# Turning the value sums back at the end of the odd visit instead of in the middle of the even one

## The chip, the core and the metric

The kernel runs on one core of a Trainium2 chip. The metric is the device time of one execution in microseconds (us); lower is better. The kernel before took 2076.41 us (median of 3 runs, 2075.64 to 2079.05).

## What is computed

Four layers act on one sequence of 2048 rows of 640 numbers, in single precision: a Fourier mixing layer, a sliding-window attention layer, and the same two again. Each adds to its input:

```python
x = x + A(layernorm(x));  x = x + B(layernorm(x))      # twice
# A: y = dft_seq_re @ (x @ dft_hid_re.T) - dft_seq_im @ (x @ dft_hid_im.T)
# B, with H = 32 heads of Dh = 20 and a window of 256 keys:
qkv = x @ wqkv
scores = einsum("bhqd,bhkd->bhqk", q, k) * Dh ** -0.5
scores = where((i - j >= 0) & (i - j < 256), scores, -1e9)
o = einsum("bhqk,bhkd->bhqd", softmax(scores), v);  y = o @ wo
```

The change concerns layer B alone, which the kernel runs twice (function `attention`).

## The kernel before

**Numbers.** Single-precision operands of the large products are split into two 16-bit parts, and three products of parts are added up, so one product over 640 inner elements is 15 matmuls of 128 rows. The matmuls of the probabilities with the values, and two transposes behind them, are single precision throughout.

**Visits.** `attention` walks over *visits*, numbered by `G` in the loop at L1315. A visit handles one tile of 128 queries and two pairs of heads; two visits in a row (an even and an odd `G`) share the same heads. Every matmul goes through the helper at L126, and inside `attention` each one is tied to the one issued before it (`in_turn`), so the tensor engine runs them in exactly the order in which the Python code calls them. That order in one visit is:

1. `scores` for the oldest key tile, into the tile `sk` (even and odd alike);
2. `by_key`: the scores once more with keys on the partitions, for a visit eight earlier, also into `sk`;
3. `scores` for the two nearer key tiles, into `sq`. Steps 1 to 3 are 24 small matmuls on 62 rows of the array;
4. in an odd visit `hand_on`: a transpose of the row maxima `tops` through a bank `pf` (the scalar engine copies it to `ht`);
5. in an even visit `back(n)` (L1244): two single-precision transposes of `pvs` (the value sums of four heads) into a bank `pf`;
6. in an odd visit `values(n, part)` (L1223): 32 matmuls of `v` with the probabilities `ptq` into a bank `pf`, which the scalar engine then copies to `pvs` (L1242);
7. `run_unit` (L1068): the *fill*, usually 15 matmuls of 128 rows that belong to other work (projections of later blocks, of 256 or 320 columns; the output product `bo`, `ot` of 320 columns), into a bank `pf`.

Value sums are made at lag `VALUE_LAG` = 11 visits (odd) and turned back at `BACK_LAG` = 12 (the even visit behind it).

**Banks.** All the `pf` tiles of steps 4 to 7 come from one pool of two banks (`new_f`, L207). Whoever takes a bank waits until its last user's result was read out: by the scalar engine (`ht`, `pvs`, `qf` L365, `v` L881) or by the vector engine (`o` L1259, `x` L935).

**The vector engine.** Per visit it masks and reduces two tiles of scores (`largest`, L1148: COPY_PREDICATED L1155 and TENSOR_REDUCE L1157, twice). Behind `back`'s transposes it takes a reciprocal (`r`, L1258) and a product (`o`, L1259), from which GpSimd writes two parts `os` (L1261, L1262). `in_line("dve")` ties an instruction behind the last one noted in `marks["dve"]`; before, only the masks and reductions note themselves there. Between these stand the *slow steps* of layer norms (lines 139 to 166), one in an even visit and two in an odd one, and the sums of output units (L935).

When the last heads of a block are turned back, output units are queued for `OUT_STEPS[0]` = 4 steps (two visits) after the current one, and the turning of `os` into `ot` (a DMA on SyncE's queue) likewise.

Of the kernel before, what the change touches and what calls it, by code (L numbers as in the profile page):

```python
# [15 lines left out]
OP = mybir.AluOpType  # L16
AX = mybir.AxisListType

S, D, H, DH, P = 2048, 640, 32, 20, 128
# [26 lines left out]
BACK_LAG = 12  # L46
# [26 lines left out]
def body(ctx: ExitStack, tc: tile.TileContext, x_in, cmat, whid, wqkv, wo, out):  # L73
    nc = tc.nc
# [749 lines left out]
    def attention(layer, proj, dst, final):  # L824
        with ExitStack() as st:
# [293 lines left out]
            TOP, PT, topped, marks = {}, {}, [None], {}  # L1119
# [103 lines left out]
            def values(n, part):  # L1223

                b, k = divmod(n, NP // 2)
                q = PT[n]
                if part == 0:
                    PVS[n] = new_f().rearrange("p (a b) -> p a b", a=4)
                pv = PVS[n]
                j = 2 * b  # L1230
                for kt, cols, sel in (((j, slice(0, 2), slice(2, 5, 2)), (j - 2, slice(0, 1), slice(0, 1))),
                                      ((j - 1, slice(0, 2), slice(1, 4, 2)), (j + 1, slice(1, 2), slice(5, 6))))[part]:
                    if kt < 0:
                        continue
                    for h in range(4):
                        hh = 4 * k + h
                        matmul(pv[32 * h:32 * h + 32, cols], VS_[kt][:, VS * hh:VS * hh + 32], q[:, h, sel],
                                         start=kt == j, stop=kt == j + 1, tile_position=(0, 32 * h), skip_group_check=True)
                if part:
                    del PT[n]  # L1240
                    PVS[n] = sb.tile([P, 2, P], F32, tag="pvs", name="pvs", bufs=2)
                    nc.scalar.activation(PVS[n], pv[:, :2], AF.Copy)  # L1242

            def back(n):  # L1244
                b, k = divmod(n, NP // 2)
                t = PVS.pop(n)
                pv = new_f().rearrange("p (a b) -> p a b", a=4)
                for m in range(2):
                    transpose(pv[:, 2 + m], t[:, m], idf)
                pbv = pv[:, 2:].rearrange("p m (h e) -> p (m h) e", e=32)  # L1250
                if k == 0:
                    flush(("out", b - 3))
                    OS[b] = sb.tile([P, 2, 2, D], F16, tag="os", name="os", bufs=3)
                r = sb.tile([P, 8], F32, tag="r", name="r", bufs=2)
                cs = slice(4 * k * DH, 4 * (k + 1) * DH)
                o = sb.tile([P, 2, 4 * DH], F32, tag="o", name="o", bufs=2)
                hi, lo = (OS[b][:, :, m, cs] for m in range(2))
                nc.vector.reciprocal(r, pbv[:, :, DH])  # L1258
                nc.vector.tensor_tensor(o.rearrange("p m (h e) -> p (m h) e", e=DH), pbv[:, :, :DH],  # L1259
                                        r.unsqueeze(2).to_broadcast([P, 8, DH]), op=OP.mult)  # L1260
                nc.gpsimd.tensor_copy(hi, o)  # L1261
                nc.gpsimd.tensor_tensor(lo, o, hi, op=OP.subtract)  # L1262
                last = b == NBQ - 1
                d1 = (k + 1) * 4 * DH // P
                if last and d1 > k * 4 * DH // P and (d1 > 2 or k > LAST_FROM):
                    for m in range(2):
                        step0 = max(now[0] + LAST_STEPS[0], NG + 2 * KEY_LAG if m else LAST_STEPS[1] if d1 < ND else 0)
                        fill.append(Unit(step0, last_out(2 * b + m, lastd[0], d1), "last", NS + 2 * d1 + m, [(2 * b + m - 2, 2)]))
                    lastd[0] = d1
                elif k == NP // 2 - 1 and not last:  # L1270
                    for m in range(2):
                        i = 2 * b + m
                        at, due, kind = now[0] + OUT_STEPS[0] + OUT_STEPS[2] * m, 2 * NP * (b + 2) + OUT_STEPS[1], ("out", b)
                        need = [(i - 2, 2)] if i > 1 else []
                        outs.append((at, need, partial(out_turn, i)))
                        fill.append(Unit(at, out_tile(i), kind, due + 3 * m + 2, [(i, 1)] + ["wo"] * (layer == 0)))
# [33 lines left out]
            def due(G, lag):  # L1310
                n, m = divmod(G - lag, 2)
                return n if m == 0 and 0 <= n < NG // 4 else None

            wanted, x2s, normed_at = [], [], [-FREE_STEPS]
            for G in range(NS // 2 + 1):  # L1315
                now[0] = g = 2 * G
                b, r = divmod(g, 2 * NP)
                if g == NG:
                    floor.append(loads[-1])
                if g < NG:  # L1320
                    if r == 0:
                        flush(("qk", b))
                        if b == 0:
                            queue_qk(1)
                            queue_v(1)
                keyed = 0 <= G - KEY_LAG < NG // 2
                if g < NG:
                    scores(G, (0,))
                if keyed:
                    by_key(G - KEY_LAG)  # L1330
                if g < NG:
                    scores(G, (2, 1))
                if g < NG:
                    largest(G, 0)
                if keyed:
                    probabilities(G - KEY_LAG, 1)
                if g < NG:
                    largest(G, 1)
                    if G % 2:
                        part_tops(G // 2)  # L1340
                if keyed:
                    probabilities(G - KEY_LAG, 0)
                n = due(G, HAND_LAG)
                if n is not None:
                    hand_on(n)
                n = due(G, BACK_LAG)
                if n is not None:
                    with in_line("dve"):
                        back(n)
                c = 2 if g == 0 else b + 3  # L1350
                if g < NG and c < NBQ and (g == 0 or r == X2_STEP):
                    wanted.append(c)
                if wanted and x2s and g >= x2s[0] + 4 * (g > 0):
                    slow.append(rows_norm(wanted.pop(0), x2s.pop()))
                    x2s.clear()
                if slow:
                    normed_at[0] = g
                if wanted and not slow and not x2s and g >= normed_at[0] + FREE_STEPS:
                    x2s += [g, [keep.tile([P, D], F32, tag="res0", name="x2", bufs=2) for t in range(2)]]
                    for t in range(2):  # L1360
                        load(x2s[1][t], x2_d[2 * wanted[0] + t])
                if g < NG and r == ROWS_STEP:
                    flush(("v", b))
                    if b < NBQ - 2:
                        proj.new_rows(b + 2)
                        queue_qk(b + 2)
                        queue_v(b + 2)
                if g < NG and r == HIDDEN_STEP:
                    if b == NBQ - 1 and not final:
                        flush(("v", b))  # L1370
                        hidden = Hidden(xu_d)
                        pieces = hidden.pieces()
                        for k in range(2):
                            fill.append(Unit(g + NEXT_STEPS[k], hidden.stage(k, None), "next", NG + k))
                for _ in range(STEPS[layer][G % 2]):
                    slow_step()
                run_later()
                for _ in range(PIECES):
                    next(pieces, None)
                while handed and handed[0][0] <= now[0]:  # L1380
                    handed.popleft()[1]()
                run_held(1 << 20)
                if outs and outs[0][0] <= g and all(done.get(k, 1 << 20) + FREE_STEPS <= g for k in outs[0][1]):
                    outs.pop(0)[2]()
                n = due(G, VALUE_LAG)
                if n is not None:
                    for part in range(2):
                        values(n, part)
                if not (G % 2 and NG - 2 * NP <= g < THIN_TO[layer]):
                    run_unit(G % 2 == 0)  # L1390
                if G % 2 and g < NG and left() and 2 * left() > must_to() - r:
                    run_unit()
            while unit[0] is not None or fill or slow or idle or later:
                now[0] += 1
                run_later()
# [37 lines left out]
```

## Time and profile before

| what | value |
|---|---|
| median of 3 runs | 2076.41 us |
| the profiled execution, whole | 2078.21 us |
| its span (first to last instruction) | 2076.4 us |
| granted tensor clock, mean | 0.998 |
| TensorE busy with matmuls | 1996.0 us (96%) |
| VectorE, GpSimd, ScalarE busy | 1552.9, 1471.0, 1114.1 us |
| attention, first layer (its first transposes of `pvs` start at 597.4 us) | about 597 to 1066 us |
| attention, second layer (from 1619.4 us) | about 1619 to 2076 us |

All times of rows are in us from the span's start unless marked ns. A timeline row gives start, length, engine, line, operation, output and inputs; "x15" means that 15 instructions in a row were merged, and the brackets give the idle time of the engine before the row and what ended it. PE is the tensor engine's matmuls, PEld its weight loads, DVE the vector engine, ACT the scalar engine, POOL GpSimd, SP the queue engine. A matmul's end is modelled in such a profile, so starts are the firmer reading.

### The profile page before, as it was taken

To read this page: it belongs to the slowest core of one execution; us is meant where nothing else is said; L and a number is where in the kernel's file an instruction comes from. 1 tells how busy PE (TensorE), PEld (TensorE's weight loads), DVE (VectorE), ACT (ScalarE), POOL (GpSimd) and SP (SyncE) were. 2 spreads that over 40 slices of the span, in tenths; PEclk is the share of its full clock that TensorE was granted. 3 is DMA by queue.
4 is the path that set the end of the run, shared out by engine and by line. 5 is a ranking of instruction groups with operands and counts; after the bars stand their busy time and mean duration, and the time that the engine had idled before them with its cause. 6 is when DMAs were issued, how large, how long until landed. Compare 5 with 4: busy or idle time off the path is not lost.

```text
span 2076.4 us, 55961 instructions
## 1 busy us (share of the span) xinstructions
PE 1996.0 (96%) x21881; PEld 1452.4 (70%) x21881; DVE 1552.9 (75%) x3261; ACT 1114.1 (54%) x1971; POOL 1471.0 (71%) x2162
## 2 busy tenths in 40 slices
PE   7999999999999999999999999999999999999998
PEld 4777777776767776777667777777677677777765
DVE  8888778767688788766638779787777877776673
ACT  5444555534256666666654444444342666666664
POOL 5777788868458778765557778777783677776654
PEclk9999999999999999999999999999999999999999
DMA  7556467565554444443635455454845454543322
GB/s 271 182 200 207 159 216 237 169 254 193 141 107 118 109 109 117 98 102 91 175 131 175 159 174 183 149 171 144 298 146 131 92 124 106 128 110 88 85 74 71
DMA packets 280509, 311.11 MB, mean 150 GB/s; under 512 B 107572, under 2 KB 214836, under 8 KB 271156
## 3 DMA queue, kind: packets, MB, share of 16 engines
q1 hardware_dynamic: 279668, 306.88, 49.9%
q8 instruction: 171, 2.80, 0.6%
q14 instruction: 94, 0.77, 0.1%
q10 hardware_dynamic: 576, 0.66, 0.1%
HBM read 201.72 MB, written 83.46 MB: 137 GB/s over the span
## 4 chain that ended last, share of the span: by engine, by line
PE 63%; DVE 16%; issue 6%; ACT 5%; POOL 5%; DMA 4%; SPq 0%; DVEq 0%; POOLq 0%; ACTq 0%
PE pf L126 28%; PE y L126 11%; PE x L126 10%; PE z L126 7%; PE sk L126 5%; DVE cc L536 4%; DVE sq L1155 3%; DVE m L1157 2%; ACT ptq L1210 2%; PE sq L126 2%; DMA res<-accd 2%; DVE res L559 1%; DVE lnt L151 1%; POOL cs L526 1%; DVE lnst L139 1%
## 5 line engine op out<-in xcount | busy, mean ns | idle before, releaser
L126 PEld LDWEIGHTS <-cc 128*128 128x128 f16 x5376 | 524.4, 98 | 214.8 <-issue 15.1
L1210 ACT ACTIVATE ptq<-sk,shift,alpha 128x768 f32<-128x768 f32 (+2 forms) x512 | 469.3, 944 | 111.0 <-DVE x L935 55.0
L126 PEld LDWEIGHTS <-big 128*128 128x128 f16 x4320 | 415.0, 98 | 129.6 <-issue 29.5
L1157 DVE TENSOR_REDUCE m<-sq 128x2 f32<-128x512 f32 (+1 forms) x512 | 345.4, 675 | 25.8
L1155 DVE COPY_PREDICATED sq<-mask,sk 128x256 f32<-128x256 int32 x448 | 189.7, 423 | 144.4 <-PE sq L126 138.1
L533 ACT ACTIVATE cc<-cs 128x512 f16<-128x512 f32 x256 | 153.6, 623 | 262.6 <-POOL cs L526 150.3
L126 PE MATMUL pf<-early,big 128*128 128x256 f16 x2400 | 289.2, 274 | 4.4 <-ACT ht L1175 3.7
L1214 POOL TENSOR_SCALAR_AFFINE_SELECT ptq<-ptq 128x512 f32<-128x512 f32 x224 | 144.3, 644 | 183.1 <-ACT ptq L1210 180.8
L126 PE MATMUL y<-zc,cc 128*128 128x320 f16 x1728 | 262.8, 299 | 3.2 <-DVE pf L559 3.2
L536 DVE SCALAR_TENSOR_TENSOR cc<-cs,cc 128x512 f16<-128x512 f32 x256 | 248.1, 978 | 6.9 <-ACT cc L533 6.8
L536 DVE SCALAR_TENSOR_TENSOR cc<-cq,cc 128x512 f16<-128x512 f32 x192 | 207.1, 1080 | 0.1
L126 PE MATMUL pf<-ptq,v 128*32 128x128 f32 (+1 forms) x3840 | 183.6, 329 | 10.1 <-DVE o L1259 3.5
L126 PE MATMUL z<-zc,cc 128*128 128x320 f16 x1152 | 177.7, 299 | 7.0 <-DVE res L559 7.0
L126 PE MATMUL x<-zc,cc 128*128 128x320 f16 x1152 | 177.7, 299 | 0.0
L1216 POOL TENSOR_SCALAR_AFFINE_SELECT ptq<-ptq 128x512 f32<-128x512 f32 x256 | 164.9, 644 | 13.0 <-ACT ptq L1210 12.8
L126 PEld LDWEIGHTS pf<-ptq,v 128*32 128x32 f32 x3840 | 114.8, 110 | 56.0 <-PE pf L126 7.7
L365 ACT ACTIVATE qf<-pf 128x256 f32<-128x256 f32 x160 | 60.9, 381 | 166.7 <-PE pf L126 128.7
L126 PE MATMUL pf<-big,early 128*128 128x320 f16 x960 | 141.0, 299 | 2.2 <-ACT ht L1175 1.3
L525 POOL TENSOR_TENSOR cs<-cq 128x512 f32<-128x512 f32 x64 | 86.6, 1354 | 69.8 <-DVE cc L536 69.1
L126 PEld LDWEIGHTS <-qs 62*128 62x128 f16 x2688 | 87.7, 94 | 59.1 <-issue 57.9
L126 PE MATMUL pf<-bo,ot 128*128 128x320 f16 x840 | 123.5, 299 | 4.6 <-DVE x L935 2.6
L126 PEld LDWEIGHTS <-ot 128*128 128x128 f16 x960 | 91.9, 98 | 46.6 <-issue 9.4
(141 smaller groups left out, 3505.4 us busy)
## 6 DMA issues: line engine op xcount, KB each, us to landing
cq<-in_cmat_dram SPq DMA_DIRECT2D x64, 1024.0 KB
accd<-res SPq DMA_DIRECT2D x96, 320.0 KB
res<-accd SPq DMA_DIRECT2D x96, 320.0 KB
x<-x2d SPq DMA_DIRECT2D x64, 320.0 KB
qkd<-early SPq DMA_DIRECT2D x160, 128.0 KB
ks<-qkd SPq DMA_DIRECT2D x108, 160.0 KB
qs<-qkd SPq DMA_DIRECT2D x84, 160.0 KB
x2d<-res SPq DMA_DIRECT2D x32, 320.0 KB
```

Of the source, the lines that this page charges most:

```text
L126: i = getattr(nc.tensor, what)(*args, **kw)
L139: nc.vector.bn_stats(st[:, h], x[:, h * 320:(h + 1) * 320])
L151: ts(u, g, g, h, op0=OP.mult, op1=OP.mult)
L365: nc.scalar.activation(f, pf[:, :QB], AF.Copy, scale=down)
L525: g.tensor_tensor(s1, a21, a22, op=OP.add)
L533: nc.scalar.activation(cc[m][:, 0], f, AF.Copy, scale=C_UP)
L536: nc.vector.scalar_tensor_tensor(cc[m][:, 1], f, C_UP, cc[m][:, 0], op0=OP.mult, op1=OP.subtract)
L1155: marks["dve"] = nc.vector.copy_predicated(near[pi][:, :, 0], mask[:, None, :].to_broadcast([P, 2, P]), far).ins
L1157: marks["dve"] = nc.vector.tensor_reduce(TOP[n][:, pi, :, k], near[pi][:, :, :1 + (i >= 1)], axis=AX.XY, op=OP.max).ins
L1210: marks["act"] = nc.scalar.activation(o[:, pi], tps[pi][:, :, first:], AF.Sigmoid, bias=shift, scale=alpha[:, 0:1]).ins
L1214: nc.gpsimd.affine_select(out=q[:, :, a0], in_=q[:, :, a0], pattern=[[0, 4], [-1, P]], base=0, channel_multiplier=1, compare_op=OP.is_gt, ...
L1216: ins = nc.gpsimd.affine_select(out=q[:, :, a0 + 2], in_=q[:, :, a0 + 2], pattern=[[0, 4], [1, P]], base=0, channel_multiplier=-1, compare ...
```

## The change

`back(n)` no longer waits for its own place in the even visit. When `values` has run in an odd visit, `n` is noted in a list; if a fill ran in that visit, `back(n)` is called at once behind it, which is ahead of the even visit's first `scores`. If no fill ran, it is called at the old place of the next even visit. The product `o` also notes itself in `marks["dve"]`, so the next visit's masks are placed behind it on the vector engine.

```diff
-                nc.vector.tensor_tensor(o.rearrange("p m (h e) -> p (m h) e", e=DH), pbv[:, :, :DH],
-                                        r.unsqueeze(2).to_broadcast([P, 8, DH]), op=OP.mult)
+                marks["dve"] = nc.vector.tensor_tensor(o.rearrange("p m (h e) -> p (m h) e", e=DH), pbv[:, :, :DH],
+                                                       r.unsqueeze(2).to_broadcast([P, 8, DH]), op=OP.mult).ins
...
+            turned_back = []
             for G in range(NS // 2 + 1):
...
-                n = due(G, BACK_LAG)
-                if n is not None:
+                if turned_back:
                     with in_line("dve"):
-                        back(n)
+                        back(turned_back.pop())
...
                     for part in range(2):
                         values(n, part)
+                    turned_back.append(n)
+                ran = False
                 if not (G % 2 and NG - 2 * NP <= g < THIN_TO[layer]):
-                    run_unit(G % 2 == 0)
+                    ran = run_unit(G % 2 == 0)
                 if G % 2 and g < NG and left() and 2 * left() > must_to() - r:
-                    run_unit()
+                    ran = run_unit() or ran
+                if ran and turned_back:
+                    with in_line("dve"):
+                        back(turned_back.pop())
```

**On the tensor engine**, in the middle of the second attention layer, around an even visit (`big` and `early` are a projection unit of the odd visit ahead of it, `bo` and `ot` the output unit of the even visit, `idf` the matrix that transposes):

```order
@@ -28359,4 +28359,5 @@
 L126 LDWEIGHTS big
 L126 MATMUL pf<-early,big 128x256
+L126 MATMUL pf<-idf,pvs 128x128 x2
 L126 LDWEIGHTS qs
 L126 MATMUL sk_22900<-ks,qs 128x128
@@ -28407,5 +28408,4 @@
 L126 LDWEIGHTS qs
 L126 MATMUL sq_22899<-ks,qs 128x128
-L126 MATMUL pf<-idf,pvs 128x128 x2
 L126 LDWEIGHTS ot
 L126 MATMUL pf<-bo_66,ot 128x320
```

The two transposes leave the place between the even scores and the even fill and stand between the odd fill and the even scores.

**On the tensor engine**, in the odd visit behind it, where the transpose of `tops` and the first value matmul take their banks; the brackets name the engines whose semaphores an instruction waits for. Before:

```order
L126 LDWEIGHTS tops_77 [waits Pool_49]
L126 MATMUL pf<-idh,tops_77 16x128 [waits DVE_49]
L126 MATMUL pf<-ptq,v 32x256 [waits DVE_49,PE_49]
L126 MATMUL pf<-ptq,v 32x256 x3
L126 MATMUL pf<-ptq,v 32x128 x4
```

And with the change:

```order
L126 LDWEIGHTS tops_77 [waits Pool_49]
L126 MATMUL pf<-idh,tops_77 16x128 [waits PE_49]
L126 MATMUL pf<-ptq,v 32x256 [waits DVE_49]
L126 MATMUL pf<-ptq,v 32x256 x3
L126 MATMUL pf<-ptq,v 32x128 x4
```

The banks change hands: before, the value sums took the bank that held the turned-back sums (a wait for the vector engine's `o`, and one for the transposes themselves); now the transpose of `tops` takes it, and the value sums take the even fill's bank and wait for its reader alone. Of the value sums that follow a transpose of `tops`, 50 carry the pair of waits before, and 8 with the change.

**On the vector engine**, in the same two visits: an odd visit's last mask and reduction, then the even visit's. Before:

```order
L1155 COPY_PREDICATED sq_22899<-mask,sk_22901 128x256
L1157 TENSOR_REDUCE m<-sq_22899 128x2
L1155 COPY_PREDICATED sq_22898<-mask,sk_22900 128x256
L1157 TENSOR_REDUCE m<-sq_22898 128x2
L1155 COPY_PREDICATED sq_22899<-mask,sk_22901 128x256
L1157 TENSOR_REDUCE m<-sq_22899 128x2
L1258 RECIPROCAL r<-pf 128x8
L935 SCALAR_TENSOR_TENSOR x_24640<-pf,beta,x_24640 128x320
L1259 TENSOR_TENSOR o<-pf,r 128x160
```

And with the change:

```order
L1155 COPY_PREDICATED sq_22899<-mask,sk_22901 128x256
L1157 TENSOR_REDUCE m<-sq_22899 128x2
L1258 RECIPROCAL r<-pf 128x8
L1259 TENSOR_TENSOR o<-pf,r 128x160
L1155 COPY_PREDICATED sq_22898<-mask,sk_22900 128x256
L1157 TENSOR_REDUCE m<-sq_22898 128x2
L1155 COPY_PREDICATED sq_22899<-mask,sk_22901 128x256
L1157 TENSOR_REDUCE m<-sq_22899 128x2
L935 SCALAR_TENSOR_TENSOR x_24864<-pf,beta,x_24864 128x320
```

The reciprocal and the product move ahead of the even visit's masks and reductions, and the output unit's sum follows the reductions directly.

## The prediction

> **What bounds the kernel now.** I read the busy times first, then the two stretches of attention, then who waits for whom, then single visits on the timeline. The page's busy line, and the sum of the windows 597 to 1040 us and 1620 to 2035 us, attention's steady parts:
>
> ```profile
> PE 1996.0 (96%) x21881; PEld 1452.4 (70%) x21881; DVE 1552.9 (75%) x3261; ACT 1114.1 (54%) x1971; POOL 1471.0 (71%) x2162
> sum 858.00, PE 829.22 PEld 611.74 DVE 643.95 ACT 568.73 POOL 601.86; mean PE 414.61 PEld 305.87 DVE 321.98 ACT 284.37 POOL 300.93
> ```
>
> The tensor engine (PE) sets the time: 829 of 858 us busy here, at full clock, while the vector engine (DVE) is busy for 644. So what counts is the distance between starts on PE. The waits, by waiter and releaser (us in total, times, longest):
>
> ```profile
> DVE sq L1155 <- PE sq L126: 155.2, 142, 2.6
> PE sq L126 <- DVE m L1157: 5.3, 9, 1.1
> PE pf L126 <- DVE o L1259: 3.5, 9, 0.7
> PEld pf L126 <- PE pf L126: 7.7, 24, 0.8
> PEld pf L126 <- DVE x L935: 3.6, 11, 0.4
> ```
>
> The masks usually wait for PE, seldom the other way round. One pair of visits on PE, from the even scores to the next even scores:
>
> ```profile
> 1693.39 0.29 PE L126 MATMUL sk<-ks,qs 62*128 62x128 f16 x4
> ...
> 1694.17 0.44 PE L126 MATMUL pf<-idf,pvs 128*128 128x128 f32 x2
> 1694.44 2.20 PE L126 MATMUL pf<-bo,ot 128*128 128x320 f16 x15
> 1696.57 0.29 PE L126 MATMUL sk<-ks,qs 62*128 62x128 f16 x4
> ...
> 1697.35 0.22 PE L126 MATMUL pf<-idh,tops 128*16 128x128 f16 x1
> 1697.61 1.51 PE L126 MATMUL pf<-ptq,v 128*32 128x256 f32 x32
> ...
> 1700.79 0.29 PE L126 MATMUL sk<-ks,qs 62*128 62x128 f16 x4
> ```
>
> Scores 0.78 us, transposes back 0.27, fill 2.13, scores 0.78, transpose of `tops` 0.26, then value sums and fill to the end: 7.40 in all, with no large gap. A change of order can win only small pieces, about 120 times.
>
> **The change, part by part.** It adds no arithmetic. By the instruction order, 105 of 128 `back`s move; the rest find no fill and stay.
>
> (a) *Transposes behind the fill.* Each moved `back` has two transposes. Behind scores they cost 0.27 (above). Where they stand between full-height matmuls:
>
> ```profile
> 1065.99 0.38 PE L126 MATMUL pf<-idf,pvs 128*128 128x128 f32 x2
> 1066.21 0.43 PE L126 MATMUL sk<-bo,ot 128*128 128x320 f16 x2
> 1066.41 0.21 DVE L1258 RECIPROCAL r<-pf 128x8 f32<-128x8 f32 x1 [3.58 <-PE pf L126]
> 1066.73 0.33 DVE L1259 TENSOR_TENSOR o<-pf,r 128x160 f32<-128x160 f32 x1
> ```
>
> 0.22: 0.05 less, so 105 x 0.05 = -5 us. Transposes directly ahead of scores are not shown; the bounds are 0 and -5. I take -5, since the 0.05 is a weight load that scores cannot hide and a fill can. [...]
>
> (b) *The pair of waits.* At 1697.35 the value sums start 0.26 after the transpose of `tops`; they are among those that wait for two engines. Where they wait for one, and where `o` is late:
>
> ```profile
> 806.59 0.22 PE L126 MATMUL pf<-idh,tops 128*16 128x128 f16 x1
> 806.60 1.51 PE L126 MATMUL pf<-ptq,v 128*32 128x256 f32 x32
> 813.46 0.22 PE L126 MATMUL pf<-idh,tops 128*16 128x128 f16 x1
> 813.94 0.31 DVE L1259 TENSOR_TENSOR o<-pf,r 128x160 f32<-128x160 f32 x1
> 814.39 1.51 PE L126 MATMUL pf<-ptq,v 128*32 128x256 f32 x32 [0.71 <-DVE o L1259]
> ```
>
> 0.01, and 0.93. So the pair costs 0.25 even where nothing is late: the row of 24 waits of weight loads for PE (7.7 us) is this. The order has 50 pairs before and 8 after: 42 x 0.25 = -10.5 us. The bounds are -10.5 and 0 (if the 0.25 is the end of the `tops` transpose itself). I take -10.5: the two kinds differ in nothing else. [...]
>
> (c) *Late results.* `o` is now made a visit earlier, so the 3.5 us of waits for it go. The value sums now wait for the reader of the even fill's bank; the scalar engine is early, but `x` (L935) is tight. The vector engine in the same even visit:
>
> ```profile
> 1694.34 0.43 DVE L1155 COPY_PREDICATED sq<-mask,sk 128x256 f32<-128x256 int32 x1 [2.04 <-PE sq L126]
> ...
> 1695.93 0.69 DVE L1157 TENSOR_REDUCE m<-sq 128x2 f32<-128x512 f32 x1
> ...
> 1696.68 0.55 DVE L935 SCALAR_TENSOR_TENSOR x<-pf,beta,x 128x320 f32<-128x320 f32 x1
> ```
>
> `x` can start when the reduction ends (1696.62) and ends at 1697.2; without the transposes (0.27) and the 0.25, value sums would start at 1697.09. So they wait some 0.15, in 31 visits by the order: 4.7 us, of which 3.6 is there already. Part (c): -3.5 + 1.1 = -2.4, bounds -3.5 and +2.
>
> (d) *A shorter even visit.* From even to odd scores PE now has no transposes, but the odd scores overwrite what the even reductions read. With a 320-column fill the odd scores come at 1696.30 instead of 1696.57 and reach `sq` 0.46 later, at 1696.76; the reductions end at 1696.62, so 0.14 is left. With a 256-column fill:
>
> ```profile
> 809.79 0.29 PE L126 MATMUL sk<-ks,qs 62*128 62x128 f16 x4
> 812.40 0.69 DVE L1157 TENSOR_REDUCE m<-sq 128x2 f32<-128x512 f32 x1
> 812.57 0.29 PE L126 MATMUL sk<-ks,qs 62*128 62x128 f16 x4
> 813.03 0.50 PE L126 MATMUL sq<-ks,qs 62*128 62x128 f16 x8
> ```
>
> The reduction ends at 813.09, just when `sq` is wanted; 0.27 earlier, PE waits for about 0.28. The order has 28 such visits: +7.8, less some 2 of the 5.3 us that PE waits for `m` today: +6, bounds 0 and +8.
>
> (e) *`r` and `o` ahead of the even masks.* This is the added wait: the masks now stand behind `o`, which waits for the transposes; behind the masks are the reductions, and for those wait the odd scores on PE. From the rows under (a), `o` ends 1066.73 + 0.33 - 1065.99 = 1.07 after the transposes start. Even scores start 0.22 to 0.35 after them (the row of 0.22, and an allowance of mine of 0.13 for going over to scores), and masks 0.95 after the scores (1693.39 to 1694.34), so `o` is done 0.1 to 0.2 early. That cover is gone where layer-norm steps stand ahead of the reciprocal, which the order shows in 33 odd visits:
>
> ```profile
> 808.89 0.14 DVE L148 TENSOR_SCALAR lnt<-lnmv 128x1 f32<-128x1 f32 x1
> ...
> 810.69 0.21 DVE L152 TENSOR_SCALAR lnt<-lnt 128x1 f32<-128x1 f32 x1
> ```
>
> Eight steps last from 808.89 to 810.90; with 0.65 for `r` and `o` behind them the masks come 0.3 to 0.5 late, and 0.14 of that is free. Some 17 visits have such long chains: 17 x 0.2 = +3, bounds 0 and +13 (33 x 0.4).
>
> *At nothing.* The transposes wait for `pvs`:
>
> ```profile
> 808.04 1.81 PE L126 MATMUL pf<-early,big 128*128 128x256 f16 x15
> 808.40 0.36 ACT L1242 ACTIVATE pvs<-pf 128x256 f32<-128x256 f32 x1
> ```
>
> The copy ends at 808.76, the fill at about 809.65: it hides the copy with 0.9 to spare; without a fill the call stays at its old place. GpSimd's two `os` parts come earlier too, and SyncE's turning of `ot` with its load of `x` goes out a visit earlier, together with the units that use them; nothing on PE waits for these queues in the rows above. At both ends of attention a few units change places; I take 0, give or take 2.
>
> Sum: -5 - 10.5 - 2.4 + 6 + 3 = -8.9 us. The rows are from an execution of 2078.21 us (span 2076.4, 1.8 around it), 0.09% above the median; taken off the median of 2076.41, the forecast is **2067.5 us**, by its own bounds 2058 to 2072.
>
> **Rivals.**
>
> *The vector engine eats it.* Costs (d) and (e) near their upper ends, 8 and 8: -17.9 + 16 = -1.9, 2074.5. For it: in visits of the kind at 809.79 both engines are just in time today. Against it: 155 us of waits of the masks for PE, most of them in even visits.
>
> *Slower: the even masks come late in every moved visit.* One mechanism: fill, transposes, `o`, masks, reductions and odd scores become one chain across PE and DVE. If the masks come d late, the 77 visits with wide fills pay d - 0.14, and the 28 others d on top of 0.28. Against -17.9 it decides from d = 0.2 (77 x 0.06 + 28 x 0.48 = 18); with d = 0.3 it is 12.3 + 16.2 - 17.9 = +11, 2087. For it: only 0.1 to 0.2 of slack by (e). Against it: 72 moved visits have nothing between the odd reduction and the reciprocal.
>
> *It doesn't do what (b) says:* the 0.25 stays, as the value sums must let the `tops` transpose end. Then -5 - 2.4 + 9 = +1.6, 2078. Against it: the start at 806.60.
>
> **How the numbers follow.** Forecast 0.64, vector engine eats it 0.18, slower 0.10, (b) fails 0.08. About 0.2% (4 us) is what a measurement of this kernel can tell from no change. Faster by more: 0.64 and a little of the first rival, 0.67. Within: the rest of it and (b), 0.21. Slower: 0.12. The range is 2055 to 2079: below, all gains and none of the costs (2076.41 - 5 - 10.5 - 3.5 - 2 = 2055.4); above, the first and the third rival; the slower one is left out.
>
> **What would show it.** Right: value sums 0.01 after `tops` in most odd visits, and no row of 24 waits of weight loads for PE; transposes to scores 0.22 to 0.35, and scores straight to fill; `PE sq` waiting for `DVE m` some 30 times for 8 to 12 us instead of 5.3; masks of even visits waiting less for PE. Wrong: waits of `sq` for `m` in most visits (the slower rival), a distance of 0.26 with one wait only (the third), or transposes that wait for `pvs`.

## The result, and the profile after

The changed kernel is slower: 2084.78 us, median of 7 runs (2081.82 to 2088.47), against 2075.64 us for the kernel before in 7 runs beside it. The ratio is 1.0039 with a 95% interval of 1.0026 to 1.0051, so about 9 us were lost where 9 were forecast as a gain. The profiled execution is the fastest of the seven (2081.82 us, span 2080.1, 3.7 more than the span before). Ratios in this document are of undisturbed executions; a single one of 4602 us in a later experiment (with the last chains back) is not in its kernel's ratio.

The waits of the changed kernel (us in total, times, longest):

```profile
DVE r L1258 <- PE pf L126: 98.4, 79, 6.1
...
DVE sq L1155 <- PE sq L126: 67.3, 160, 2.3
...
PE pf L126 <- POOL os L1261: 5.2, 2, 4.6
...
PE pf L126 <- DMA ot<-os: 4.2, 1, 4.2
...
PE sq L126 <- DVE m L1157: 3.3, 8, 0.7
```

The vector engine now waits in front of `r` rather than in front of the masks (67.3 us there, 155.2 before), as the move intends. The row of 24 weight loads that waited for PE and the waits of `pf` for `o` are gone. PE's waits for `m` went down, not up. But TensorE has rows that the kernel before did not have: it waits for `os` from GpSimd and for the DMA that turns `os` into `ot`, once for over 4 us each.

The move itself does what it should. One pair of visits of the changed kernel on PE, of the same kind as the pair shown before (even scores, output product, odd scores, `tops`, value sums, fill, transposes):

```profile
1698.02 0.28 PE L126 MATMUL sk<-ks,qs 62*128 62x128 f16 x4
...
1701.71 0.22 PE L126 MATMUL pf<-idh,tops 128*16 128x128 f16 x1
1701.72 1.51 PE L126 MATMUL pf<-ptq,v 128*32 128x256 f32 x32
...
1704.81 0.38 PE L126 MATMUL pf<-idf,pvs 128*128 128x128 f32 x2
1705.13 0.28 PE L126 MATMUL sk<-ks,qs 62*128 62x128 f16 x4
```

From even scores to even scores it takes 7.11 us, where it took 7.40. The value sums start 0.01 behind `tops` instead of 0.26; over both layers 88 of 119 do so, where 40 did before.

So the loss is not spread over the visits. The place of it shows when the same value sums are followed through both kernels. The 63rd, 64th, 74th and 75th group of value sums, before:

```profile
1056.38 1.51 PE L126 MATMUL pf<-ptq,v 128*32 128x256 f32 x32
...
1062.51 1.51 PE L126 MATMUL pf<-ptq,v 128*32 128x256 f32 x32
...
1675.13 1.50 PE L126 MATMUL pf<-ptq,v 128*32 128x256 f32 x32
...
1682.28 1.51 PE L126 MATMUL pf<-ptq,v 128*32 128x256 f32 x32
```

and in the changed kernel (the first row begins within its group):

```profile
1048.99 1.29 PE L126 MATMUL pf<-ptq,v 128*32 128x256 f32 x24
...
1061.72 1.51 PE L126 MATMUL pf<-ptq,v 128*32 128x256 f32 x32
...
1672.22 1.51 PE L126 MATMUL pf<-ptq,v 128*32 128x256 f32 x32
...
1686.14 1.52 PE L126 MATMUL pf<-ptq,v 128*32 128x256 f32 x32
```

The change is 7.4 us ahead at the 63rd group, of which 1.8 were there at the first group (591.68 against 593.48), ahead of any moved transposes; so the first layer had gained 5.6. One visit pair later it is only 0.8 ahead, a step of 6.6. In the second layer it is 2.9 ahead at the 74th and 3.9 behind at the 75th, a step of 6.8. A third step of 3.3 lies at about 2041 to 2050. Stretches around the three places, in the changed kernel (us; busy time and instructions of PE, PEld, DVE, ACT and POOL; granted clock; DMA share and GB/s):

```profile
1040.00:1070.00 30.00, 23.25 (x249) 14.51 (x247) 4.64 (x15) 8.84 (x15) 13.03 (x20) 0.94 0.25 84
1670.00:1690.00 20.00, 15.85 (x215) 11.05 (x214) 13.28 (x37) 8.96 (x15) 8.87 (x21) 0.83 0.64 127
2036.00:2056.00 20.00, 15.89 (x207) 9.98 (x202) 2.61 (x8) 10.81 (x15) 7.48 (x15) 0.91 0.25 67
```

and before:

```profile
1040.00:1070.00 30.00, 27.42 (x329) 17.83 (x327) 7.14 (x21) 14.54 (x25) 18.45 (x29) 1.00 0.30 91
1670.00:1690.00 20.00, 19.73 (x304) 14.73 (x301) 17.95 (x51) 13.39 (x22) 15.89 (x34) 1.00 0.60 129
2036.00:2056.00 20.00, 17.33 (x231) 11.21 (x231) 3.61 (x10) 11.85 (x17) 8.40 (x16) 1.00 0.28 87
```

Two things differ: PE is busy for 4.2, 3.9 and 1.4 us less, and what it does there runs partly at a lower granted clock (0.94, 0.83, 0.91 against 1.00 everywhere). The first place, on PE and then on GpSimd:

```profile
1052.61 0.38 PE L126 MATMUL pf<-idf,pvs 128*128 128x128 f32 x2
1057.59 0.23 PE L126 MATMUL pf<-idh,os 128*128 128x128 f16 x1 [4.59 <-POOL os L1261]
```

```profile
1052.23 1.26 POOL L525 TENSOR_TENSOR cs<-cq 128x512 f32<-128x512 f32 x1
1053.45 1.26 POOL L527 TENSOR_TENSOR cs<-cq 128x512 f32<-128x512 f32 x1
1054.67 1.26 POOL L526 TENSOR_TENSOR cs<-cs,cq 128x512 f32<-128x512 f32 x1
1056.01 1.26 POOL L528 TENSOR_TENSOR cs<-cq,cs 128x512 f32<-128x512 f32 x1
1057.21 0.32 POOL L1261 CAST os<-o 128x160 f16<-128x160 f32 x1
```

The last output chain of the layer (`last_out`, queued by `back` for one step after the current one) became ready one visit earlier, directly behind the transposes. It needs `os`, and the `os` part stands in GpSimd's queue behind four products for the next Fourier layer, 1.26 us each. `o` was ready at 1053.67 (a row of DVE of 0.33 us from 1053.34), so 3.5 us of the wait are this queue; the rest is the way from the transposes to `o` and the cast itself. At the second place PE waits for a turning that SyncE issued at 1674.69; the chain of waits gives it 5.89 us until it landed:

```profile
1676.09 0.39 PE L126 MATMUL sq<-ks,qs 62*128 62x128 f16 x8
1680.63 4.18 PE L126 MATMUL pf<-bo,ot 128*128 128x320 f16 x15 [4.15 <-DMA ot<-os]
```

```profile
1674.69 5.89 DMA ot<-os
```

The product behind the wait took 4.18 us at a granted clock of 0.50, where the same 15 matmuls took 2.20 at 1.00 before (from 1686.85): that is the low clock. At the third place the longest wait is of another kind, 2.05 us for the exponentials of the scalar engine (1.68 before), with a stretch at half clock behind it; two waits for `os`, of 0.66 and 0.23, follow.

### The profile page after: what moved, and what is told of

Read it like the earlier page. It is cut to its first block, busy times and chain, and to the rows that moved or that the text cites. A ratio compares the mean times of both kernels' runs of the same rounds, so it can differ in the third digit from the quotient of the medians.

```text
span 2080.1 us, 55799 instructions
## 1 busy us (share of the span) xinstructions
PE 1989.7 (96%) x21881; PEld 1450.5 (70%) x21881; DVE 1562.8 (75%) x3261; ACT 1112.3 (53%) x1971; POOL 1469.3 (71%) x2162
## 4 chain that ended last, share of the span: by engine, by line
PE 68%; DVE 14%; ACT 5%; issue 5%; DMA 4%; POOL 3%; SPq 0%; DVEq 0%; ACTq 0%; POOLq 0%
PE pf L126 30%; PE y L126 12%; PE x L126 11%; PE z L126 8%; PE sk L126 5%; DVE cc L536 3%; ACT ptq L1210 3%; PE sq L126 2%; DVE sq L1155 2%; DVE m L1157 2%; DMA res<-accd 1%; DVE res L559 1%; DMA accd<-res 1%; DVE lnt L151 1%; DVE lnst L139 1%
## 5 line engine op out<-in xcount | busy, mean ns | idle before, releaser
L126 PE MATMUL pf<-bo,ot 128*128 128x320 f16 x840 | 128.1, 306 | 8.7 <-DMA ot<-os 4.2
```

The lines of the kernel that those rows point to most:

```text
L126: i = getattr(nc.tensor, what)(*args, **kw)
```

## The experiments

**Theory A**: the moved order gains about what was forecast, and the loss comes from the output work. `back` sets its times from the current step; called one visit earlier, it sends the turning, the output products and the last chains one visit earlier too. TensorE then waits for GpSimd and SyncE, and after each wait it runs at half clock for a while. **Theory B**: the moved transposes, `r` and `o` cost it themselves, by late masks.

**The move and the times, apart.** Four kernels. The first keeps the move and restores the times (`now[0]` is twice the visit's number, so `now[0] % 4` adds one visit in an odd visit and nothing in an even one):

```diff
+                at0 = now[0] + now[0] % 4
-                        step0 = max(now[0] + LAST_STEPS[0], ...
+                        step0 = max(at0 + LAST_STEPS[0], ...
-                        at, due, kind = now[0] + OUT_STEPS[0] + ...
+                        at, due, kind = at0 + OUT_STEPS[0] + ...
```

> The change with the times of the output work put back: where the move calls back in the odd visit, the turning of a block's output, its two output products and the two last output chains are given the visit that they had before the change, so that only the transposes of the sums with r, o and the os parts stand earlier. Theory A (the output work that goes out one visit earlier makes TensorE wait for GpSimd and for the DMA that turns os, 4.59 us at 1053, 4.15 us at 1676 and 2.05 us at 2041, and each of these waits is followed by a stretch at half clock of 3.4 or 6.8 us): the steps of +6.6, +6.8 and about +3 us of the changed kernel go, the waits of TensorE for os and for ot shrink from 19 to under 4 us together, and the time is 2066 to 2071 us, 5 to 10 below the kernel before. Theory B (the moved transposes with r and o cost it themselves, by masks that come late on the vector engine): the time stays at 2081 to 2088 us.

The second is the kernel before with only the times made early (`now[0] - 2` in both places, also for the twelve groups that the change leaves in the even visit):

> The kernel before, with the transposes left in the even visit, and only the times of the output work set one visit earlier, as the change has them by its move. Theory A: the waits for os and ot and the half clock behind them come back without the move; slower than the kernel before by 8 to 16 us, 2084 to 2092 us. Theory B: nothing but the order of a few output products moves, 2074 to 2078 us.

The third and the fourth restore one of the two times each, with the move (the third `at`, the fourth `step0`):

> The change with the times put back for the turning and the products of the ordinary blocks only (the wait of 4.15 us for the DMA at 1676 us in the second layer); the two last chains of each layer keep their earlier start. Theory A: the step of +6.8 us goes and those at the ends of the two layers stay, 2075 to 2080 us. Theory B: 2081 to 2088 us.

> The counterpart of the kernel that kept only the last chains early: here the last two output chains of each layer get the visit back that they had before the change, and the turning and the products of the ordinary blocks stay one visit early, as the change has them. If the two parts of the loss add, this kernel gives back what the other kept (about 9 us from 2078.4 to 2069.4, by the waits of 4.59 us for os and the half clock behind), and stands at 2073 to 2078 us; the wait of 4.15 us for the DMA at 1676 us is there, none of over 1 us for os. If the half clock after the turning depends on where the wait falls and it shows none here, 2070 to 2073 us. If the last chains cost nothing, 2082 to 2087 us.

Measured, each against runs of the kernel before on the same chip:

| transposes | last chains | turning and products | us | ratio to before (95%) |
|---|---|---|---|---|
| moved | old visit | old visit | 2069.40 | 0.9970 (0.9957 to 0.9982) |
| old place | early | early | 2090.26 | 1.0073 (1.0057 to 1.0090) |
| moved | early | old visit | 2078.37 | 1.0011 (0.9998 to 1.0024) |
| moved | old visit | early | 2075.66 | 0.9994 (0.9985 to 1.0003) |
| moved | early | early (the change) | 2084.78 | 1.0039 (1.0026 to 1.0051) |

Theory B falls, and of A it holds that the early times lose. They cost about 15 us without the move (0.0073 x 2075) and about 14 with it (1.0039 - 0.9970); the move gains about 6 with the old times and 7 with the early ones (1.0073 - 1.0039). The two parts of the loss add, as far as the intervals tell (some 3 to 4 us either way): about 8.5 us for the last chains and 5 for the turning. In the trace of the first kernel no row of PE waiting for `os` is left; of the waits for the turning there is this:

```profile
PEld L126 <- DMA ot<-os: 0.4, 1, 0.4
```

It is faster than both the kernel before and the change. GpSimd's queue is the same there, but the product that needs `os` comes behind it:

```profile
1056.80 1.28 POOL L528 TENSOR_TENSOR cs<-cq,cs 128x512 f32<-128x512 f32 x1
1058.03 0.32 POOL L1261 CAST os<-o 128x160 f16<-128x160 f32 x1
1059.86 0.22 PE L126 MATMUL pf<-idh,os 128*128 128x128 f16 x1
```

The steps at the 64th and 75th group are gone. Of the third, 1.6 us stay: the wait of 2.05 us for the exponentials and the half clock behind it are there with the old times too, so this part comes with the move itself and not, as the expectation had it, from the output work. In the second kernel the wait for `os` is 4.6 us again, with a step of 6.65; the wait for the turning is 1.8 us, with no half clock behind it, and a step of 1.9. That trace is of its fastest execution (2084.78 us), so the rest of the 15 us is not placed.

**The waits, taken away another way.** If the waits are the cause and not the order of the output products, removing them with the early times kept must help. The first kernel leaves PE's order of the change untouched and makes the last `os` parts of the first layer elsewhere:

```diff
-                nc.gpsimd.tensor_copy(hi, o)
-                nc.gpsimd.tensor_tensor(lo, o, hi, op=OP.subtract)
+                eng = nc.vector if last and not final and k > LAST_FROM else nc.gpsimd
+                eng.tensor_copy(hi, o)
+                eng.tensor_tensor(lo, o, hi, op=OP.subtract)
```

> The change as it stands, with TensorE's instructions in the very same order; only the os parts of the last four groups of the first layer are made by the vector engine instead of GpSimd, where the trace shows four products by the coefficients of the next stage (1.26 us each) queued ahead of them. Theory (the last chains lose because TensorE waits behind GpSimd's queue): the wait of 4.59 us falls to about 1.2 us (0.21 and 0.33 for r and o, and two copies of 0.2 to 0.3 by the vector engine), the half clock behind it goes, and the time falls by 4 to 6 us from the changed kernel's 2084.8, to 2079 to 2081 us (1.001 to 1.002 of the kernel before). Rival (the order of the output products itself loses): the time stays within 1 us of 2084.8 (1.004).

The second gives one output product a later start; the third has both edits:

```diff
-                done[i, 1] = now[0] + TURN_LAG
+                done[i, 1] = now[0] + TURN_LAG + 2 * (final and i == 0)
```

> The change with one number: in the second layer the first output product waits one visit longer for its turned tile, whose turning still goes out at the early time. Theory: the wait of 4.15 us at 1676 us for the DMA and the 6.8 us at half clock behind it go, 5 to 7 us less than 2084.8: 2078 to 2080 us (1.001 to 1.002 of the kernel before). Rival (the loss is in the other turnings, which all go out early): within 1 us of 2084.8.

> The two edits above together, all other output work at the early times of the change. Theory: with both waits gone it stands 9 to 13 us under the changed kernel, at 2071 to 2076 us, faster than the kernel before, and near the 2069.4 us of the kernel with the old times. Rival (early output work loses in more places than these two): 2079 us or more.

They came out at 2080.46 us (1.0026, 1.0012 to 1.0040), 2079.45 (1.0023, 1.0014 to 1.0032) and 2078.20 (1.0018, 1.0009 to 1.0028). All three are nearer to the kernel before than the change, but by some 3, 3 and 4 us only, with intervals that overlap its own (the third's hardly), and the third missed its figure: it did not become faster than the kernel before. The first two lie within their figures, but by luck, for the waits that they were to remove did not go. The traces show why. With `os` on the vector engine, on PE and then on DVE:

```profile
1060.49 0.23 PE L126 MATMUL pf<-idh,os 128*128 128x128 f16 x1 [1.88 <-DVE os L1263]
1061.79 0.23 PE L126 MATMUL pf<-idh,os 128*128 128x128 f16 x1 [1.07 <-DVE os L1264]
```

```profile
1059.25 1.18 DVE L1263 CAST os<-o 128x160 f16<-128x160 f32 x1
1060.47 1.27 DVE L1264 TENSOR_TENSOR os<-o,os 128x160 f16<-128x160 f32 x1
```

The wait of 4.59 became two of 1.88 and 1.07, since the two parts took 1.18 and 1.27 us and not 0.2 to 0.3; the half clock behind them stayed (0.91 from 1050 to 1070). With PE's order untouched, the step at the 64th group went from 6.6 to 4.65 us, which is the two waits and half of the 3.4 us at half clock: it is the wait that costs there, not the order. With the later product the wait for the turning is gone, but it comes back in another place, on PE and in SyncE's queue:

```profile
1692.46 0.39 PE L126 MATMUL sk<-ks,qs 62*128 62x128 f16 x3 [3.67 <-DMA qs<-qkd]
```

```profile
1681.60 2.69 SPq L196 DMA_TRANSPOSE ot<-os  x1
...
1685.64 1.95 SPq L188 DMA_DIRECT2D qs<-qkd  x2
```

The early turning holds SyncE's queue for 2.69 us ahead of the loads of `qs`, for which the next scores wait 3.67 us. With the old times the loads of the same visits go out first (1671.61 and 1672.23, the turning at 1673.48). In the third kernel this wait is 2.47 us, with no half clock behind it, and the step 2.3 us; in the second it is 4.5, against 6.8 in the change. So it is not the one product that loses: the turning itself stands one visit too early in SyncE's queue.

**What a wait costs.** The kernel with the move and the old times, with ten set stalls (one execution):

```diff
+                for c in range(COPIES[layer].get(n, 0)):
+                    t2 = sb.tile([P, 2, P], F32, tag="pvs2", name="pvs2", bufs=2)
+                    nc.vector.tensor_copy(t2, t)
+                    t = t2
```

> The kernel with the move and the output work at its old visits, and ten set stalls of TensorE: ahead of the transposes of ten chosen groups, five in each layer, the vector engine copies the sums 6, 8, 10, and so on up to 24 times from one tile to the next, so that TensorE waits for some 1 to 9 us, by an estimate of 0.3 to 0.4 us a copy. Theory (a stall costs its own length, and besides about 1.7 us, half of a stretch of 3.41 us, when TensorE has been busy for less than about half of such a stretch): each stall over about 2 us is followed by one stretch at 0.5, a stall over 5 us by one or two, and the value sums after it stand later by the stall and 1.5 to 3.5 us more; stalls under 1.5 us by their length alone. Rival (the half clock costs nothing, other waits take it up): each step is the stall's length to within 0.5 us.

Three of the ten stalls on PE, two in the first layer and one in the second (line numbers are one higher here):

```profile
801.41 0.41 PE L127 MATMUL pf<-idf,pvs 128*128 128x128 f32 x2 [3.98 <-DVE pvs L1250]
...
936.45 0.66 PE L127 MATMUL pf<-idf,pvs 128*128 128x128 f32 x2 [6.82 <-DVE pvs L1250]
...
1851.70 0.41 PE L127 MATMUL pf<-idf,pvs 128*128 128x128 f32 x2 [3.54 <-DVE pvs L1250]
```

By the second layer's stalls a copy cost 0.33 us (2.23 us of stall for 6 copies, 6.17 for 18). All ten, with the step by which the first value sums behind the stall, against the last ones ahead of it, stand later than in the kernel without stalls, and the time at half clock that lies behind the stall's end (worked out from the two traces):

```
stall us      2.23  3.54  3.98  4.41  4.85  5.51  6.17  6.82  9.83  10.49
step us       2.4   3.7   5.8   6.4   6.4   8.6   8.2   9.6   11.7  12.3
half clock us 0     0     3.4   4.7   3.0   6.3   4.5   5.6   4.1   4.0
```

The step is the stall, plus half of the half-clock time that follows, to within 0.4 us in every case; the rival (the stall alone) falls in eight of ten. The two without half clock, 2.23 and 3.54 us, cost only themselves. The stalls from 6.82 us on had three stretches at half clock, not two, the first of them within the stall, and the one of 4.41 had two. That the one of 3.54 us had none goes against "over about 2 us is followed by one": what counts is where the stall lies, told in the last section.

**Two variants of the kernel with the old times.** The move brings one call ahead that flushes an output product of an earlier block (`flush(("out", b - 3))` in `back`), so two fills stand in a row. The first variant leaves those groups in the even visit, the second leaves all groups behind the last scores of a layer (`g < NG` added to the condition of the early call).

> As the first kernel of this group, and besides the transposes of a block's first four heads stay in the even visit where their call would put an output product of an earlier block behind the fill of the odd visit (so two fills in a row without scores between). Theory A: as the first kernel, 2066 to 2071 us, and not more than 2 us from it; if the two fills in a row cost their vector wait, 1 to 3 us faster than it. Theory B: 2081 to 2088 us.

> The kernel with the move and with the output work at its old visits, and besides no transposes moved in the visits after the last scores of a layer, where the trace shows two groups of twelve products by key in a row and a wait of 2.05 us (1.66 us before the change) for the exponentials, with a half clock behind it. Theory: the wait there goes back to 1.66 us, the half clock behind it is gone, and the time falls by 1 to 3 us, to 2066 to 2069 us. Rival: the few transposes there count for nothing, within 1 us of 2069.4.

They came out at 2071.83 us (0.9984, 0.9973 to 0.9994) and 2070.49 us (0.9964, 0.9952 to 0.9977). The first is not faster, so the two fills in a row cost nothing that can be seen; whether it is slower than 0.9970 the intervals don't tell. In the second the wait of 2.05 us went back to 1.68, with no half clock behind it, as expected; a gain of 1 us lies within the intervals, and is open.

## Why the prediction was wrong

The step that failed is the paragraph *At nothing*: GpSimd's `os` parts and SyncE's turning go out a visit earlier, "together with the units that use them; nothing on PE waits for these queues in the rows above". That no row waits shows only that the margin was not used up at the old times; it was not measured. The margin could have been read in the kernel before, on SyncE's queue and on PE:

```profile
1681.76 2.25 SPq L196 DMA_TRANSPOSE ot<-os  x1
1686.85 2.20 PE L126 MATMUL pf<-bo,ot 128*128 128x320 f16 x15 [0.15 <-ACT qf L365]
```

The output product that lost used its tile 5.09 us after the turning went out; how long the turning takes, the kernel before shows only as less than that. In the changed kernel it wanted the tile at 1676.48 (1680.63 less the wait of 4.15), 1.79 us after the turning went out, and the turning took 5.89. So the units and what they need did not move together: against the 74th value sums the product moved up by 7.5 us and the turning by 4.2, and at the first place GpSimd's four products still stood ahead of `os`. By the five kernels of the table this is worth some +14 us against "0, give or take 2". The upper of its "own bounds", 2072, is not the sum of the terms' upper bounds either: that is +23 us, 2099, so even the listed terms left room for a loss.

A second term was missing altogether: the sum counted durations at full clock. By the set stalls, the wait at 1053 costs 4.59 and half of the 3.4 us behind it, 6.3 of the 6.6 measured; the one at 1676 costs 4.15 and half of the 5.6 us that lie behind its end, 6.9 against 6.8.

The terms of the sum, from the mean distances between starts on PE in both layers (worked out from the visits of attention, in the kernel before and in the one with the move and the old times):

```
distance                                        before   moved
tops to value sums, 119 times                   0.221    0.087
transposes to what follows                      0.274    0.314   (medians)
fill of an odd visit to what follows            1.744    1.648   (medians, 256 columns)
even scores to fill                             0.775    0.834
256-column fill of an even visit to scores      1.843    1.925
```

- (a) holds. Fill and transposes together take 1.962 us up to the scores, where the fill alone took 1.744: the transposes cost 0.218 there against 0.274 before, 0.056 each, of which the even fill gives back 0.011. The forecast was 0.05. The reason given fits the rows: behind scores the first transpose's weights begin to load at 1694.16, just ahead of its matmul (1694.17), behind the fill at 1704.70, 0.11 ahead (1704.81). Going from full-height matmuls to scores has a price in the traces: the first weights of the scores load 0.20 us after the start of the last full-height matmul, where full-height matmuls follow each other after 0.11. But that is paid once in either order (1700.59 to 1700.79 behind the fill before, 1704.92 to 1705.12 behind the transposes now), so the saving stands beside it.
- (b) and (c) hold: 119 x 0.134 = 15.9 us less between `tops` and value sums, against 10.5 and 3.5; some 5 of it come back in the value sums' own waits, which (c) put at 1.1.
- (d) was too dear: PE waits for `m` 8 times and 3.3 us in all, not 30 times and 8 to 12; the fill's distance grew by 0.08, about 2 us instead of 6.
- (e) is of the right size: the even scores take 0.06 more, some 5 us in 89 visits, against 3. The 0.13 in it for going over to scores was the author's estimate; by the medians it was 0.09 (0.314, against the row of 0.22).
- Together with the old times the move gives 6 us (2075.15 to 2069.40), against the forecast 8.9. In those runs the mean granted clock is 0.9973, before 0.9987; by an estimate from that (0.0014 x 2068) 2.9 us of half clock are to be taken off the gain, perhaps since the shorter visits come sooner to waits that do not get shorter, like the one of 2.05 us (1.68 before). It is an upper bound, for part of the half clock lies within the waits.
- The rival that was to make it slower, late even masks in every moved visit, is not what happened: 160 waits of masks for PE are left. That the change was slower at all had 0.12, nearly all of it on that rival and none on the queues.

## What to carry to other kernels

When a call is moved, follow every time that it sets from "now": the queued work moves by whole steps, while its inputs move only by what the call itself gained. An empty row of waits says nothing of the margin, so measure the distance from issue to use before a queue is costed at nothing. And price a stall of TensorE of some microseconds at its length plus half of the half-clock time behind it (here 0 to 6.3 us behind stalls of 2.2 to 10.5).

## What the runs showed of the hardware

**In these runs the granted clock dropped in fixed stretches.** In all twelve traces it drops to 0.5 in stretches of 3.413 us or multiples (the last one of a trace cut by its end), whose starts lie on one grid (in the changed kernel 638.3, 1058.1, 1679.4 and 2044.6, that is 123, 305 and 412 stretches apart, within 0.04 of whole numbers). Laid over all of them, the next stretch goes with PE's busy share of a full-clock one: under 0.40 busy, the next was at half clock in 36 of 36; from 0.40 to 0.60 in 13 of 106; above 0.60 in none. Between 0.40 and 0.60 the share alone does not tell. So a stall of 2.05 us was enough where it fell within one stretch (0.42 busy), and one of 3.54 was not where the grid cut it in two (0.47 and 0.49).

**Small output parts took longer on the vector engine beside GpSimd's products.** In the kernel with `os` on the vector engine, casts of the same shape from three of the four groups (the fourth took 0.24 too):

```profile
1044.86 0.24 DVE L1263 CAST os<-o 128x160 f16<-128x160 f32 x1
1052.36 0.24 DVE L1263 CAST os<-o 128x160 f16<-128x160 f32 x1
1059.25 1.18 DVE L1263 CAST os<-o 128x160 f16<-128x160 f32 x1
```

GpSimd ran nothing beside the first two, and its products of 1.26 us (from 1059.07 and 1060.29) beside the third and the part behind it; the kernel with both edits shows the same 0.24, 0.24 and 1.18. So the layout of `os` is not the reason; what differs is GpSimd's products beside it. `r` and `o`, which read a bank, took their usual 0.21 and 0.32 us beside the product that began at 1057.85. What the two engines share is not shown by these runs.
